# State products of K and V joined to the scores in one TensorE group, with a new order of work, in an mLSTM and hidden-layer kernel

## The chip, the cores and the metric

The kernel runs on one core of one Trainium2 chip. The metric is the device time in microseconds of one execution, taken as the median of several; lower is better. PE is the matrix engine (its weight loads are listed as PEld), DVE, ACT and POOL are the vector, scalar and GpSimd engines, and SP issues the transfers.

## The reference

Two parts follow each other. The first is a gated recurrence (mLSTM) over 768 steps for 4 batches and 8 heads of 40 elements; the second takes its output as 3072 tokens of 320 elements through a hidden layer of 2048.

```python
m_new = np.maximum(f_gate[:, :, t] + m, i_gate[:, :, t])
f_stab = np.exp(f_gate[:, :, t] + m - m_new)
i_stab = np.exp(i_gate[:, :, t] - m_new)
C = f_stab[:, :, None, None] * C + i_stab[:, :, None, None] * np.einsum('bhd,bhe->bhde', vt, kt)
n = f_stab[:, :, None] * n + i_stab[:, :, None] * kt
h_tilde = np.einsum('bhde,bhe->bhd', C, qt)
denom = np.maximum(np.abs(nq), 1.0)          # nq: n times qt
y[:, :, t] = o * h_tilde / denom             # o: sigmoid of o_gate
...
h = x @ w_in
g = h * np.clip(h + 3.0, 0.0, 6.0) / 6.0
return (g @ w_out).astype(np.float32)
```

The weights arrive as 64-bit floats, and the kernel decodes them into 32-bit ones on the chip.

## The kernel before, in words

**Tiling.** The recurrence is computed in chunks of 128 steps: 6 chunks a batch, 24 in all, each in two halves of four heads. Three chunks make a unit (u = 0 to 7), and a unit has two tasks, one for each four heads. For each chunk of a task there are these jobs:

- `state` (L547): the state product of K and the weighted V of the chunk, four pairs of matrix products into a PSUM bank of its own (tile `c`, L559). DVE and POOL then make the new state `C` from the old one: POOL multiplies by the decay (L567), DVE adds (L569).
- `gate` (L574): the decay matrix `gw`. For the first two chunks it is made on PE by products with a selector `sel` (tile `gb`, L589) and a minimum with a mask on DVE (L591); for all others, four rows `gsc` are fetched by a broadcast transfer (L596) and masked on POOL (L598). ACT then takes the exponential, one head at a time (L603).
- `front` (L607): scores of q and k (L624) and q times the old state (L627), both into one bank (tile `s`). DVE multiplies the scores by `gw` (L632) and the state part by `eG` (L638). From task 4 on (PT = 4) the product is split into three bf16 parts (L643 to L650).
- `back` (L657): the product with V into tile `o`, in fp32 before task PT (L669) and as 16 bf16 products from it on (L671 to L674), added into `ht` on DVE.

`fin` (L691) normalises, multiplies by the output gate, transposes on PE (tile `x`, L726) and writes the unit's input of the hidden layer as a high and a low part, `xh` and `xl`.

**Hidden layer.** For every unit there are 16 hidden blocks `h` (`mm1`, L825, eight products of 384 columns each), each followed by the activation on ACT (L839) and DVE (L841), and, for two blocks at a time, the second product into three accumulators `acc` (`mm2`). Unit 0 uses fp32 weights `vr` there (L866), the others high and low parts (L868 to L870). The low part of `g` is made by ACT and DVE (L353, L849).

**Weights.** There are 8 slices of `w_in` (`yi`) and 8 of `w_out` (`yo`); `weight_slice` (L741) decodes one: ACT scales both halves (L752, L754), DVE clamps (L757), shifts (L759) and merges sign and bits (L761), and POOL adds the low half (L766 for `vr`, L768 for `yi`). From `yi` the parts `whi`, `wlo` and `wtl` follow.

**Order.** All engines work through lists that are fixed when the program is built. A planner (class `Plan`) draws them up: every job has a due time (`due`, with the constants from `SPAN` to `FIN0`), asks in turn for an engine with an assumed cost, and the planner gives an engine to the job that is due first of those that can start. In front of the hidden layer it fills PE with dummy products `pw` (`warm`, L373), as a job of lowest rank, or of the highest where the columns of the last 3.4 us fall below `RATE`. The letter at each place of `ENGINES` says which engines an operation may go to. Waits in the lists are on semaphores, so an engine whose next entry isn't ready stands still, with all that follows it.

## Time and profile before

| | |
|---|---|
| median of 3 runs | 510.04 us (509.13 to 510.32) |
| the profiled execution | 509.07 us |
| its span in the profile | 507.3 us |
| PE, DVE, ACT, POOL busy | 499.5, 355.2, 300.4, 159.3 us |
| first hidden product starts | 50.34 us |
| last product starts | 503.62 us |
| dummy products `pw` | 363 |

The span runs from the first to the last instruction of the program; the device time has some 1.8 us around it. A row of the timeline gives start, duration, engine, line, what is written from what is read, shapes and count; matrix products overlap, so the distance between two starts, not the duration, is what one costs PE. An fp32 product has two records.

### The profile page before, as it was taken

The page shows a single profiled execution, that of the slowest core. Times are in us where ns is not written, and L with a number is a line of the kernel's source. Part 1 is how long each engine was busy: PE and PEld are TensorE (multiplying, and loading weights), DVE is VectorE, ACT ScalarE, POOL GpSimd, SP SyncE. Part 2 cuts the span into 40 slices and gives each one's busy share as a digit, 9 for nine tenths or more (in the row PEclk, how much of TensorE's full clock was granted, in tenths as well). Part 3 has the DMA queues.
Part 4 walks back from the last instruction along what each step waited for, and adds up shares of the span by engine and source line. Part 5 has one row for each costly group of instructions (what it writes and reads, how often), then busy time and mean ns, then how long its engine had stood idle before and what let it go on. Part 6 is the DMA issues. An engine that isn't in the chain of part 4 may idle for free.

```text
span 507.3 us, 10993 instructions
## 1 busy us (share of the span) xinstructions
PE 499.5 (98%) x4293; PEld 463.4 (91%) x4293; DVE 355.2 (70%) x754; ACT 300.4 (59%) x649; POOL 159.3 (31%) x195
## 2 busy tenths in 40 slices
PE   8998999999999999999999999999999999999997
PEld 8998877878999999999999999999999999999996
DVE  7879999999856776666767775765866676743332
ACT  4755566767566765657655766647665664443333
POOL 4552454465433333314431333304331331000000
PEclk9998999999999999999999999999999999999999
DMA  8755755624131532215120432215221310001001
GB/s 290 253 219 160 258 196 199 231 81 122 64 103 63 141 109 74 78 44 168 63 97 33 137 111 74 84 42 165 79 82 23 121 61 1 1 0 40 1 1 40
DMA packets 25332, 52.13 MB, mean 103 GB/s; under 512 B 2624, under 2 KB 9088, under 8 KB 25280
## 3 DMA queue, kind: packets, MB, share of 16 engines
q1 hardware_dynamic: 25280, 51.42, 31.5%
q8 instruction: 34, 0.56, 0.4%
q14 instruction: 18, 0.15, 0.1%
HBM read 47.38 MB, written 4.03 MB: 101 GB/s over the span
## 4 chain that ended last, share of the span: by engine, by line
PE 86%; DVE 8%; DMA 2%; issue 2%; ACT 1%; POOL 1%; SPq 0%; DVEq 0%; POOLq 0%
PE h L825 34%; PE acc L868 11%; PE acc L870 10%; PE acc L869 10%; PE s L624 5%; PE pw L373 3%; PE acc L866 3%; PE c L559 2%; PE s L627 2%; PE x L726 1%; PE o L671 1%; PE o L673 1%; DMA gw<-gsc 1%; DVE wlo L784 1%; DVE g L841 1%
## 5 line engine op out<-in xcount | busy, mean ns | idle before, releaser
L839 ACT ACTIVATE g<-h,half 128x384 f32<-128x384 f32 x128 | 74.0, 578 | 86.0 <-PE h L825 84.9
L841 DVE SCALAR_TENSOR_TENSOR g<-g,h 128x384 f32<-128x384 f32 x128 | 70.3, 550 | 63.7 <-ACT g L839 62.9
L868 PE MATMUL acc<-vh,gh 128*128 128x320 f32 x336 | 107.2, 319 | 0.0
L870 PE MATMUL acc<-vh,gl 128*128 128x320 f32 x336 | 104.1, 310 | 0.0
L869 PE MATMUL acc<-vl,gh 128*128 128x320 f32 x336 | 104.0, 310 | 0.0
L849 DVE TENSOR_TENSOR gl<-g,gh 128x384 fp32r<-128x384 f32 x112 | 74.8, 668 | 32.8 <-ACT gh L353 32.2
L825 PE MATMUL h<-xh,whi 128*128 128x384 f32 x256 | 94.5, 369 | 0.1
L825 PE MATMUL h<-xh,wlo 128*128 128x384 f32 x256 | 86.6, 338 | 0.0
L825 PE MATMUL h<-xl,whi 128*128 128x384 f32 x256 | 86.5, 338 | 0.0
L353 ACT CAST gh<-g 128x384 fp32r<-128x384 f32 x112 | 57.2, 511 | 43.2 <-DVE g L841 42.3
L650 POOL TENSOR_TENSOR p<-gw,p 128x512 bf16<-128x512 f32 x36 | 44.4, 1232 | 103.0 <-ACT p L353 96.8
L603 ACT ACTIVATE gw<-gw,cT 128x128 f32<-128x128 f32 x192 | 65.7, 394 | 14.4 <-POOL gw L598 11.9
L598 POOL TENSOR_SCALAR_AFFINE_SELECT gw<-gw 128x512 f32<-128x512 f32 x46 | 33.9, 736 | 110.7 <-DMA gw<-gsc 99.9
L868 PEld LDWEIGHTS acc<-vh,gh 128*128 128x128 f32 x336 | 63.1, 188 | 0.9
L869 PEld LDWEIGHTS acc<-vl,gh 128*128 128x128 f32 x336 | 63.2, 188 | 0.0
L870 PEld LDWEIGHTS acc<-vh,gl 128*128 128x128 f32 x336 | 63.1, 188 | 0.0
L353 ACT CAST p<-gw 128x512 bf16<-128x512 f32 x72 | 44.3, 615 | 19.9 <-DVE gw L632 17.7
L825 PEld LDWEIGHTS h<-xh,whi 128*128 128x128 f32 x256 | 48.0, 188 | 4.4 <-DVE g L841 1.2
L825 PEld LDWEIGHTS h<-xl,whi 128*128 128x128 f32 x256 | 48.3, 189 | 0.2
L825 PEld LDWEIGHTS h<-xh,wlo 128*128 128x128 f32 x256 | 48.1, 188 | 0.0
L825 PE MATMUL h<-xh,wtl 128*128 128x384 f32 x128 | 43.3, 338 | 0.0
L825 PE MATMUL h<-xl,wtl 128*128 128x384 f32 x128 | 43.2, 338 | 0.0
(104 smaller groups left out, 884.1 us busy)
## 6 DMA issues: line engine op xcount, KB each, us to landing
st<-in_qk_dram SPq DMA_DIRECT2D x48, 256.0 KB, 2.7
gw<-gsc SPq DMA_DIRECT2D x46, 256.0 KB, 3.3
nat<-in_nat_dram SPq DMA_DIRECT2D x16, 492.0 KB, 4.4
rawi<-in_w_in_dram SPq DMA_DIRECT2D x8, 640.0 KB, 6.0
rawo<-in_w_out_dram SPq DMA_DIRECT2D x8, 640.0 KB, 4.7
on<-in_on_dram SPq DMA_DIRECT2D x8, 480.0 KB, 3.7
out_dram<-ob SPq DMA_DIRECT2D x24, 160.0 KB, 2.2
f_s<-in_fg_dram SPq DMA_DIRECT2D x1, 96.0 KB, 2.1
```

Of the source, the lines that this page charges most:

```text
L353: nc.scalar.copy(dst, src)
L598: nc.gpsimd.affine_select(gw, gw, pattern=[[0, 4], [1, L]], compare_op=ALU.is_ge, fill=NEG, base=0, channel_multiplier=-1)
L603: nc.scalar.activation(gw[:, h, :], gw[:, h, :], AF.Exp, bias=cT[:, c, r0 + h : r0 + h + 1], scale=1.0)
L624: nc.tensor.matmul(sp[:, z, hs], st[rows, 1, hs], st[rows, 0, hs], start=True, stop=True)
L650: E(e).tensor_sub(p[:, 2], gw, p[:, 1])
L825: nc.tensor.matmul(hp, w, x, start=n == 0, stop=n == len(seq) - 1)
L839: nc.scalar.activation(g, hp, AF.Relu, bias=half, scale=1.0 / 6.0)
L841: nc.vector.scalar_tensor_tensor(g, g, 1.0, hp, ALU.min, ALU.mult)
L849: E(e).tensor_sub(gl, g, gh.bitcast(F32))
L868: nc.tensor.matmul(acc, gh[:, ts_], VH[f // 4][:, f % 4, :], start=f == 0, stop=False)
L869: nc.tensor.matmul(acc, gh[:, ts_], VL[p][:, f % 2, :], start=False, stop=False)
L870: nc.tensor.matmul(acc, gl[:, ts_], VH[f // 4][:, f % 4, :], start=False, stop=f == NF - 1)
```

## The change

The state product moves. From unit 1 on (`MS = 1`), `state` is no longer a job of its own: `front` issues the four state products (`outer`), directly ahead of the scores, into 84 free columns of the scores' bank, and makes the new state from there (`update`) behind its two DVE operations; only then is the bank given back. The update is two DVE operations that multiply and add at once, where POOL multiplied and DVE added.

The gate matrices of the first 7 chunks in order, instead of 2, are made on PE. The mask comes in by one more product there, of 512 bf16 columns, and ACT reads PSUM directly, so that the DVE minimum is gone.

Decoding a weight slice takes no add on POOL any more: the low half is scaled to its place by ACT, and two DVE operations shift and merge bits. Weighting V may go to ACT too. `PT` is 6 instead of 4, so tasks 4 and 5 keep fp32 products with V.

The planner's picture of PE is another: a cost for each change of kind (`CHANGE`), a bonus for staying with attention work (`STICK`), a later due time for `back` (`BKO`), waits by the engine that released, and new values of nearly all constants. The lists are therefore in another order everywhere. The file also allows units of other sizes; the list used is eight times three, as before.

On PE, in unit 2 of the hidden layer, around the state product of task 7, chunk 1 (`c7_1` before; `h2_3` is hidden block 3 of unit 2, `o7_0` a product with V), the list before reads

```order
L825 MATMUL h2_3_2595<-xh2_1927,wtl_77 128x384
L825 MATMUL h2_3_2595<-xl2_1928,wtl_77 128x384
L559 MATMUL c7_1_2635<-vp7_2375,nat7_2372 64x42 x4
L825 MATMUL h2_4_2684<-xh2_1927,whi_75 128x384
L825 MATMUL h2_4_2684<-xl2_1928,whi_75 128x384
```

and now

```order
L894 MATMUL h2_6_2499<-xh2_1679,wtl_77 128x384
L894 MATMUL h2_6_2499<-xl2_1680,wtl_77 128x384
L610 MATMUL s7_1_2533<-vp7_2326,nat7_2315 64x42 x4
L693 MATMUL s7_1_2533<-st7_1_1796 128x128 x4
L696 MATMUL s7_1_2533<-C7_0_2456,st7_1_1796 128x42 x4
L743 LDWEIGHTS p7_0_2463
L743 MATMUL o7_0_2547<-vb7_2327,p7_0_2463 128x84
```

The state product stood alone between two hidden blocks; it now writes into the scores' tile and the scores follow it, and behind them the product with V of the chunk before.

On PE in the start-up, the first gate matrices (`gb`), the list before reads

```order
L589 MATMUL gb0_0_187<-g_s_97,sel_102 128x128 x4
L452 MATMUL pl0_226<-gTs_99,last_98 128x32
L624 MATMUL s0_0_159<-st0_0_108 128x128 x4
L589 MATMUL gb0_1_219<-g_s_97,sel_102 128x128 x4
L430 MATMUL pc1_234<-ident_78,i_s_94 128x32
```

and now

```order
L652 MATMUL gb0_0_220<-mask_102,identb_103 128x512
L654 MATMUL gb0_0_220<-g_s_97,sel_101 128x128 x4
L693 MATMUL s0_0_154<-st0_0_108 128x128 x4
L502 MATMUL pc0_205<-gTs_99,last_98 128x32
L652 LDWEIGHTS identb_103
L652 MATMUL gb1_0_221<-mask_102,identb_103 128x512
L654 MATMUL gb1_0_221<-g_s_97,sel_101 128x128 x4
```

Each gate has a mask product ahead of its four selector products, and the second gate is that of task 1.

On DVE, where the hidden layer of unit 0 begins (`yo` and `yi` are weight slices, `g0_0` the first hidden block's activation, `xl0` the last part of its input), the list before reads

```order
L732 TENSOR_TENSOR xl0_651<-x2_1_2_949,xh0_650 128x128
L638 TENSOR_TENSOR ht2_787<-s2_1_886,eG_82 128x168
L761 SCALAR_TENSOR_TENSOR yi3_522<-rawi3_434,yi3_522 128x640
L757 TENSOR_SCALAR yo0_847<-yo0_847 128x640
L757 TENSOR_SCALAR yi4_934<-yi4_934 128x640
L759 TENSOR_SCALAR yo0_847<-yo0_847 128x640
L759 TENSOR_SCALAR yi4_934<-yi4_934 128x640
L841 SCALAR_TENSOR_TENSOR g0_0_1013<-g0_0_1013,h0_0_998 128x384
```

and now

```order
L804 TENSOR_TENSOR xl0_503<-x2_1_2_911,xh0_502 128x128
L849 TENSOR_TENSOR wtl_77<-yi3_559,wtl_77 64x128
L850 TENSOR_TENSOR wtl_77<-yi3_559,wtl_77 64x128
L829 TENSOR_SCALAR yo1_746<-yo1_746 128x640
L852 TENSOR_TENSOR wlo_76<-yi3_559,whi_75 128x2x256
L831 SCALAR_TENSOR_TENSOR rawo1_640<-yo1_746,rawo1_640 128x640
L829 TENSOR_SCALAR yi4_800<-yi4_800 128x640
L910 SCALAR_TENSOR_TENSOR g0_0_974<-g0_0_974,h0_0_962 128x384
```

At the same point one slice of each kind more is decoded, and the three DVE operations of a slice are a clamp and two merges.

The diff, cut to its core:

```diff
-SWITCH = 0.12
+SWITCH = 0.13
+MS = 1
+BKO = 9.255
+CHANGE = {"moe": 0.085, ("moe", "front"): 0.092, ("moe", "state"): 0.092, ("back", "front"): 0.085, ("fin", "front"): 0.095, ("back", "state"): 0.085, ("fin", "state"): 0.095, ("front", "moe"): 0.105, ("state", "moe"): 0.106}
+STICK = 39.626
-PT = 4
-GB = 2
+PT = 6
+GB = 7
-GP = [1, 1, 4]
+GP = [1, 2, 3]
-RATE = 3500
+RATE = 4500
...
+                if e == "p" and self.last != "moe" and j["gen"].__name__ not in ("mm1", "mm2", "warm"):
+                    due -= STICK
...
-                    if big and self.small:
-                        cost = cost + 0.08
+                    if kind != self.last:
+                        cost = cost.plus(CHANGE.get((self.last, kind), CHANGE.get(kind, 0.0)))
...
+    def outer(task, cp, cps):
+        for h in range(4):
+            z, j = divmod(h, 2)
+            nc.tensor.matmul(cps[z * HR : z * HR + HR, j, :], tasks[task]["kn"](cp, h), tasks[task]["vp"][:, cp, h, :], start=True, stop=True)
+
+    def update(task, cp, cps):
...
+            q0 = (r0 // 4) * 2
+            yield "d", 0.33
+            for k in range(2):
+                nc.vector.scalar_tensor_tensor(Cn[:, k, :], cur[:, k, :], dec[:, c, q0 + k : q0 + k + 1], cps[:, k, :], ALU.mult, ALU.add)
...
-                nc.tensor.matmul(cps[z * HR : z * HR + HR, j, :], T["kn"](cp, h), T["vp"][:, cp, h, :], start=True, stop=True)
...
-                e = yield psub(16, 84)
-                q0 = (r0 // 4) * 2
-                E(e).tensor_tensor(Cn, cur, dec[:, c, q0 : q0 + 2, None].broadcast_to([128, 2, E2]), ALU.mult)
-                yield "d", cd(84)
-                nc.vector.tensor_add(Cn, Cn, cps)
...
+            nc.tensor.matmul(src, GT["identb"], mask[:, None, :].broadcast_to([128, 4, L]), start=True, stop=False)
             for h in range(4):
-                nc.tensor.matmul(pb[:, h, :], sel[:, h, :], g_s[:, c * L : (c + 1) * L], start=True, stop=True)
-            yield "d", cd(512)
-            nc.vector.tensor_tensor(gw, pb, mask[:, None, :].broadcast_to([128, 4, L]), ALU.min)
-            put(*gb)
+                nc.tensor.matmul(src[:, h, :], sel[:, r0 + h, :], g_s[:, c * L : (c + 1) * L], start=False, stop=h == 3)
...
+        both = u >= MS and c < NC - 1
+        cost = pair(4, L).plus(SWITCH) if cur is None else pair(4, L) + pair(4, E2).plus(SWITCH)
+        yield "p", KV + cost if both else cost
+        if both:
+            cps = sp[:, 0, 2 * L + 2 * E2 : 2 * L + 4 * E2].rearrange("p (j e) -> p j e", j=2)
+            outer(task, cp, cps)
...
+        if both:
+            yield from update(task, cp, cps)
         put(*got)
+        if u >= MS:
+            event(f"state{nm}")
...
-        e = yield pick(15, d=lf(WC), g=1.0)
-        E(e).tensor_scalar(y, y, 3, None, ALU.logical_shift_left)
-        yield "d", ld(WC)
-        nc.vector.scalar_tensor_tensor(y, hw, 0x80000000, y, ALU.bitwise_and, ALU.bitwise_or)
-        yield "g", cg(WC)
+        yield "d", Lock(0.765)
+        nc.vector.scalar_tensor_tensor(lw, y, 3, lw, ALU.logical_shift_left, ALU.bitwise_or)
...
-            nc.gpsimd.tensor_tensor(VR[i].rearrange("p a d -> p (a d)"), y, lw, ALU.add)
-        else:
-            nc.gpsimd.tensor_tensor(y, y, lw, ALU.add)
+        yield "d", Lock(0.765)
+        nc.vector.scalar_tensor_tensor(VR[i].rearrange("p a d -> p (a d)") if kind == "o" else y, hw, 0x80000000, lw, ALU.bitwise_and, ALU.bitwise_or)
```

More of the change, by code (lines that the diff above doesn't have):

```diff
@@ L139, in add @@
         self.n += 1
-        self.waiting.append(dict(due=due, n=self.n, gen=gen, t=0.0, eng=None, req=None, after=list(after), att=att, slack=DELTA if slack is None else slack, first=slack is not None, hot=hot))
+        j = dict(due=due, n=self.n, gen=gen, t=At({}), eng=None, req=None, after=list(after), need=set(after), att=att, slack=DELTA if slack is None else slack, first=slack is not None, hot=hot)
+        self.left += 1
+        for a in j["need"]:
+            self.waiting.setdefault(a, []).append(j)
+        if not j["need"]:
+            self.fresh.append(j)
     def put(self, tag, slot):
@@ L212, in ready @@
     def ready(self, j, e, cost):
[L213 removed]
+        start = self.free[e]
+        for o, t in j["t"].by.items():
+            t += (HOPS if e in "dag" else 0.0) if o == e else HOPP if e == "p" and j["att"] and o != "t" else HOP
+            if t > start:
+                start = t
         if e == "g" or isinstance(cost, Lock):
@@ L267, in run @@
             self.settle()
-        assert not self.waiting, [(w["n"], w["due"], w["after"]) for w in self.waiting]
+        assert not self.left, sorted(self.waiting)
 def ca(n):
@@ L375, in mlstm_moe_kernel @@
     GT = {k: early["ea"].tile(sh, F32, name=k) for k, sh in dict(
-        f_s=[BH, S], i_s=[BH, S], m_s=[BH, S], lf=[BH, S], g_s=[128, S], last=[128, 128], gTs=[128, NC, BH], mask=[128, L], one=[BH, L], sel=[128, 4, L]).items()}
+        f_s=[BH, S], i_s=[BH, S], m_s=[BH, S], lf=[BH, S], g_s=[128, S], last=[128, 128], gTs=[128, NC, BH], one=[BH, L], sel=[128, 8, L]).items()}
+    GT.update({k: early["ea"].tile([128, L], BF16, name=k) for k in ("mask", "identb")})
     def load_ident():
@@ L855, in mm2 @@
         native = u < NV
-        for t in range(U):
+        for t in range(UNITS[u]):
             if p == 0:
@@ L975, in _layout @@
     vp[..., D] = 1.0
+    kc, vc = chunks(k), chunks(vp)
+    both = np.concatenate([kc, vc], 3)
+    nat = units(both, lambda a: np.stack([np.concatenate([a[:, q, :, : 4 * D].transpose(1, 0, 2).reshape(L, -1), a[:, q, :, 4 * D :].transpose(1, 0, 2).reshape(L, -1)], 1) for q in range(2)]))
     w1, w2 = moe_w_in.view(np.int64), moe_w_out.view(np.int64)
```

402 lines of the change are left out of this document (227 added, 175 removed).

## The prediction

> **What bounds the kernel now.** I read the page's shares first, then the stretches of the span, then the chain that ended last.
>
> ```profile
> PE 499.5 (98%) x4293; PEld 463.4 (91%) x4293; DVE 355.2 (70%) x754; ACT 300.4 (59%) x649; POOL 159.3 (31%) x195
> ...
> PE 86%; DVE 8%; DMA 2%; issue 2%; ACT 1%; POOL 1%; SPq 0%; DVEq 0%; POOLq 0%
> ```
> ```profile
> 0.00:49.50 49.50, 46.59 (x627) 43.60 (x628) 40.22 (x114) 27.60 (x73) 22.95 (x38) 0.97 0.70 235
> 49.50:110.00 60.50, 58.94 (x387) 48.99 (x385) 57.99 (x114) 41.16 (x79) 30.50 (x28) 1.00 0.59 199
> 110.00:507.30 397.30, 393.93 (x3284) 370.80 (x3282) 256.95 (x529) 231.65 (x498) 105.84 (x131) 1.00 0.23 72
> ```
>
> The columns of the second fence are PE, PEld, DVE, ACT, POOL, clock, DMA share and GB/s. There are three stages. Up to 50 us the attention of unit 0 is prepared and PE is filled up with dummy products; DVE is busy 40 of 49.5 us. From 50 to 110 us the hidden layer of unit 0 runs while the weights are still being decoded; PE (58.9 of 60.5) and DVE (58.0) are both full. After 110 us only PE counts: it loses nothing until the final copy and store. So the time is (start of the first hidden product) + (PE work behind it) + (waits of PE) + (the tail behind the last product). The start is at 50.34 us:
>
> ```profile
> 48.74 1.53 PE L373 MATMUL pw<-ones 128*128 128x128 bf16 x19
> 50.34 0.44 PE L825 MATMUL h<-xh,whi 128*128 128x384 f32 x1
> ```
>
> **The joined state products.** Busy rows overlap on PE, so I price by distances between starts. A state product that stands alone between hidden products reads:
>
> ```profile
> 186.63 0.34 PE L825 MATMUL h<-xh,wtl 128*128 128x384 f32 x1
> 186.81 0.34 PE L825 MATMUL h<-xl,wtl 128*128 128x384 f32 x1
> 187.08 0.44 PE L559 MATMUL c<-vp,nat 128*64 128x42 f32 x8
> 187.45 0.44 PE L825 MATMUL h<-xh,whi 128*128 128x384 f32 x1
> 187.73 0.34 PE L825 MATMUL h<-xl,whi 128*128 128x384 f32 x1
> ```
>
> Hidden products follow each other at 0.175 us (186.63 to 186.81 is one such step). Going into the state product takes 0.27, so 0.095 more; the state product itself 0.37; the first hidden product behind it takes 0.28, so 0.105 more. Standing alone costs 0.20 us. Where before happens to have state and scores next to each other:
>
> ```profile
> 107.83 0.44 PE L559 MATMUL c<-vp,nat 128*64 128x42 f32 x8
> 108.20 0.72 PE L624 MATMUL s<-st 64*128 64x128 f32 x8
> 108.75 0.54 PE L627 MATMUL s<-C,st 64*128 64x42 f32 x8
> 109.22 0.44 PE L825 MATMUL h<-xh,whi 128*128 128x384 f32 x1
> 109.50 0.34 PE L825 MATMUL h<-xl,whi 128*128 128x384 f32 x1
> ```
>
> the state product is again 0.37 and the scores' 0.55 is not lengthened, so the join is free. Behind the first hidden product the old order has 32 state products, 29 of them with dense work next; the new one has 32, all with scores next: 29 x 0.20 = -5.8 us. The other kinds are regrouped too: attention pieces between dense work fall from 107 to 70, so 8 more go than the 29. They are mostly P x V products, which now stand behind the scores. One of them saves about its exit and that of the scores in front, 0.1 each, and some of this is given back where scores used to follow P x V: -1.0 us for these, an estimate between 0 and -1.6 (8 x 0.20). Together -6.8.
>
> The Trainium skill, TensorEngine Tiling (Array Packing), Tiling Modes, says that a change of tiling mode drains TensorE, and state product (128x64) and scores (64x128) are different modes; by that rule 32 joins would each pay a change again, about 3.2 us at the 0.10 of the rows. The trace does not agree: 107.83 to 108.75 shows no such time.
>
> **P x V of two more tasks in fp32.** Tasks 4 and 5 leave the bf16 split.
>
> ```profile
> 51.85 0.98 PE L669 MATMUL o<-nat,gw 128*128 128x42 f32 x8
> 52.66 0.42 PE L825 MATMUL h<-xh,whi 128*128 128x384 f32 x1
> ...
> 181.21 0.21 PE L671 MATMUL o<-vb,p 128*128 128x84 bf16 x1
> ...
> 181.81 0.71 PE L624 MATMUL s<-st 64*128 64x128 f32 x8
> ```
>
> 0.81 us against 0.60, of which 0.08 is the change to scores: +0.29 x 6 = +1.7 on PE. The casts and subtractions that go leave ACT, DVE and POOL, which have room there. One chunk's scores (0.55 and 0.47 by 108.20 to 109.22) and one P x V (0.81) move ahead of the first hidden product: -1.8 behind it. These two cancel: -0.1.
>
> **The start.** Seven gate matrices are now made on PE instead of two.
>
> ```profile
> 6.59 1.11 PE L589 MATMUL gb<-g_s,sel 128*128 128x128 f32 x8
> 7.61 0.38 PE L452 MATMUL pl<-gTs,last 128*128 128x32 f32 x2
> ...
> 17.93 6.03 PE L373 MATMUL pw<-ones 128*128 128x128 bf16 x105
> 23.89 0.44 PE L559 MATMUL c<-vp,nat 128*64 128x42 f32 x8
> ...
> 42.17 0.72 PE L373 MATMUL pw<-ones 128*128 128x128 bf16 x10
> 44.03 1.09 PE L669 MATMUL o<-nat,gw 128*128 128x42 f32 x8 [1.14 <-DVE C L569]
> ...
> 46.83 1.91 PE L373 MATMUL pw<-ones 128*128 128x128 bf16 x16
> 48.53 0.42 PE L726 MATMUL x<-ident,on 128*128 128x128 f32 x1
> ```
>
> Five more gates at 1.02 are +5.1. Seven mask products of 512 bf16 columns have no row; 128 columns cost 0.057 (5.96 / 105), so four times that, 0.22, is the lower end and twice that (half clock) the upper; at 0.22 they are +1.6. The chunk moved forward is +1.8. Dummy products fall from 363 to 270: -93 x 0.057 = -5.3. With the waits of before, PE would start at 50.3 + 3.2 = 53.5. Those waits are some 4 us: about 3 us in all stood idle (1.14 here, 0.31 for the first scores, the rest in pieces), and the 16 dummy products from 46.83 run at 0.106, half clock, which over 46 to 49.3 us lost 1.5. With none of it the start is 49.2. The gate path is what I expect to shorten them: the chain of waits holds a gate's DMA that starts at 30.41 and lasts 5.33 us, and then POOL and ACT.
>
> ```profile
> 30.41 5.33 DMA gw<-gsc
> ```
>
> The gates of unit 0 no longer go that way. DVE decides against it: in the part before the start it has five weight slices begun or done (three operations each) instead of four, and the add that POOL did is now a DVE operation.
>
> ```profile
> 50.46 0.49 DVE L757 TENSOR_SCALAR yo<-yo 128x640 f32<-128x640 f32 x1
> 50.86 1.88 DVE L757 TENSOR_SCALAR yi<-yi 128x640 f32<-128x640 f32 x1
> 52.66 0.48 DVE L759 TENSOR_SCALAR yo<-yo 128x640 uint32<-128x640 uint32 x1
> ...
> 54.17 0.81 DVE L761 SCALAR_TENSOR_TENSOR yo<-rawo,yo 128x640 uint32<-128x640 uint32 x1
> 54.96 0.55 DVE L841 SCALAR_TENSOR_TENSOR g<-g,h 128x384 f32<-128x384 f32 x1
> ```
>
> By 0.40 and 0.8 per operation that is +4.4, and the rest of DVE's list before the start is about even. DVE's idle time there, 49.5 - 40.2 = 9.3 us, must take this; 3.6 of it lies before the first gate data. So DVE gives 49 to 54.7, the same bracket as PE. I take 51.5, the middle: +1.2.
>
> **Waits behind the start.** Per slice DVE now does 0.40 + 0.8 + 0.8 instead of 0.40 + 0.40 + 0.8: +0.4 for 11 or 12 slices. But POOL loses its adds:
>
> ```profile
> L766 POOL TENSOR_TENSOR vr<-yo,rawo 128x640 uint32<-128x640 uint32 x8 | 13.5, 1685 | 15.2 <-issue 5.3 <-ACT whi L353 3.1 <-ACT rawo L754 2.9
> L768 POOL TENSOR_TENSOR yi<-yi,rawi 128x640 uint32<-128x640 uint32 x8 | 13.3, 1667 | 9.1 <-DVE yi L761 8.2 <-ACT gw L603 0.8
> ```
>
> 26.8 us of POOL go, and with them the hold-ups of DVE such as the 1.88 at 50.86 (its twin at 50.46 took 0.40), which ran beside a POOL add. The chain no longer passes POOL between decode and second product either. PE's row for 49.5 to 110 leaves 1.6 us idle, and with what its overlapping ends hide I put the waits of this stage at 1.9; I take 1.0 now, bounds 0 and 4 (0.4 x 11 not hidden at all). Elsewhere, three hidden blocks in a row occur four times more, and the third waits:
>
> ```profile
> 474.55 0.34 PE L825 MATMUL h<-xl,wtl 128*128 128x384 f32 x1
> 474.80 0.45 PE L825 MATMUL h<-xh,whi 128*128 128x384 f32 x1
> 475.08 0.34 PE L825 MATMUL h<-xl,whi 128*128 128x384 f32 x1
> ```
>
> 0.25 + 0.28 against 2 x 0.175 is +0.18, four times +0.7. Sum of waits -0.2. The state update is now two DVE operations behind the gate product and holds the only score bank longer, by about 0.3 (nearest row: the C add, 0.24 busy); scores are some 8 us apart in the last stage, so this is hidden there. End of the program: the same order of the last products and stores, nothing.
>
> **Sum.** 507.3 - 6.8 - 0.1 + 1.2 - 0.2 = 501.4 us of span. The profiled execution took 509.07, 1.8 more than its span: 503.2. The median of the runs is 510.04, about 1 above the profiled one: 504.
>
> **Rivals.** *The start is late.* The waits stay and PE falls to half clock once more: start at 53.5 + 1.7, time 504 + 3.7 = 507.7. For it: fewer dummy products, DVE with more work. Against: the gate DMAs go. The 1.7 is the loss of one such piece like 46 to 49.3 us. The Trainium skill, TensorE: Matmul & The Clock Gate, Part 1, gives a window of about 3.4 us after which an idle PE is put to half rate; the rows at 46.83 agree with such a length.
>
> *The join is not free.* Entry or exit is paid again inside the group, 32 x 0.1: 504 + 3.2 = 507.2, the change doing half of what it says. For it: only three joins stand behind the start in the trace. Against: they, and four ahead of the start, are all at 0.37.
>
> *Slower: the shared bank.* State product and scores wait together for the weighted V and for the one score bank, which DVE frees only after the update. Between 50 and 110 us DVE is full; if each of the nine groups there makes PE wait 1.1 us (as the P x V at 44.03 waited 1.14 for a state update), that is +10: 514. It turns the sign above 0.6 us per group. For it: DVE 58.0 of 60.5. Against: POOL's load goes, and DVE's list from the start to the last slice is no longer than before: it has fewer weight slices left and 14 of the hidden layer's `g` operations in it instead of 17.
>
> *Better.* Start at 49.2 and no waits to 110 us: 500.7.
>
> **Chances.** Forecast 0.60 (its own range 501.5 to 506.5), late start 0.12, join not free 0.07, these two together (504 + 3.7 + 3.2 = 510.9) 0.07, shared bank 0.07, better 0.07. The predicted time is 504; the range, 500.5 to 508.5, leaves out the two together and the shared bank. A measurement can tell 0.2%, so no change is 509.0 to 511.1: faster 0.60 + 0.12 + 0.07 + 0.07 = 0.86, same 0.07, slower 0.07.
>
> **What would show it.** Right: the first hidden product at 50 to 53; state product to scores 0.37 and scores unchanged; no idle PE behind 110 us; POOL nearly empty in 50 to 110. Wrong: a start above 54 (the start step), more than 0.4 us from state product to scores (the join), PE waits at scores for DVE's state update (the bank).

## The result, and the profile after

The changed kernel takes 505.82 us (median; 505.24 to 506.39), the kernel before, run beside it, 509.64 us (509.13 to 510.32): ratio 0.9924, 95% interval 0.9904 to 0.9944. A second series gave 505.72 us and 0.9932 (0.9911 to 0.9952). It is faster by 3.8 us. The forecast was 504.0 from 510.04, so 6 us. The profiled execution took 505.40 us, its span is 503.7 us. The page of the changed kernel (busy time, then the shares of the chain that ended last, by engine and by line), the chain of the kernel before by line, and the three stretches of the changed kernel (PE, PEld, DVE, ACT, POOL, granted clock, DMA share, GB/s):

```profile
PE 494.5 (98%) x4199; PEld 465.3 (92%) x4199; DVE 356.1 (71%) x839; ACT 262.3 (52%) x606; POOL 95.2 (19%) x117
...
PE 82%; DVE 5%; DMA 5%; ACT 3%; POOL 2%; issue 1%; POOLq 0%; SPq 0%; ACTq 0%; DVEq 0%
PE h L894 31%; PE acc L937 9%; PE acc L939 9%; PE acc L938 9%; PE s L693 5%; DMA gw<-gsc 5%; PE acc L935 4%; PE o L741 3%; PE s L696 3%; PE s L610 2%; PE x L798 2%; PE pw L424 1%; ACT gw L666 1%; PE o L743 1%; PE gb L654 1%
```
```profile
PE h L825 34%; PE acc L868 11%; PE acc L870 10%; PE acc L869 10%; PE s L624 5%; PE pw L373 3%; PE acc L866 3%; PE c L559 2%; PE s L627 2%; PE x L726 1%; PE o L671 1%; PE o L673 1%; DMA gw<-gsc 1%; DVE wlo L784 1%; DVE g L841 1%
```
```profile
0.00:50.50 50.50, 47.46 (x616) 44.38 (x616) 42.86 (x128) 32.13 (x92) 12.88 (x23) 1.00 0.71 228
50.50:110.00 59.50, 58.01 (x365) 49.36 (x366) 54.01 (x113) 39.12 (x81) 4.74 (x7) 1.00 0.58 186
110.00:503.70 393.70, 389.04 (x3220) 371.57 (x3218) 259.20 (x599) 191.07 (x435) 77.62 (x87) 1.00 0.24 72
```

PE's work has gone down, and GpSimd is nearly empty from 50 to 110 us (4.7 us busy, 30.5 before). But in the chain PE's share fell from 86 to 82%, and `DMA gw<-gsc`, the fetch of a gate matrix from DRAM, rose from 1% to 5%. Behind 110 us PE now leaves 4.7 us idle (393.70 - 389.04); before, 3.4, which was the tail. The overlapping ends of PE's rows hide most of its waits.

The join itself reads as forecast. One group of the changed kernel, on PE:

```profile
136.32 0.34 PE L894 MATMUL h<-xl,wtl 128*128 128x384 f32 x1
136.59 0.44 PE L610 MATMUL s<-vp,nat 128*64 128x42 f32 x8
136.96 0.71 PE L693 MATMUL s<-st 64*128 64x128 f32 x8
137.50 0.54 PE L696 MATMUL s<-C,st 64*128 64x42 f32 x8
137.98 0.30 PE L741 MATMUL o<-nat,gw 128*128 128x42 f32 x1
```

State product to scores 0.37 us, scores 0.54, as in the old trace where the two happened to be neighbours.

To part work from waiting I took, for every block of PE (products of one kind in a row), the distance from its start to the next block's start, less the usual distance for that block between those neighbours in the kernel before. What is left over counts as waiting; the rest of the time between the first hidden product and the last product is PE work. Kernels with the same products in the same order come out at the same PE work within 0.1 us, which is how far this can be trusted. All kernels of this study, each from its one profile, the time and ratio from all its runs:

| kernel | time, us | ratio to before (95%) | first hidden product | PE work behind it | waits to 110 us | waits 110 to 440 us |
|---|---|---|---|---|---|---|
| before | 509.64 | 1 | 50.3 | 450.5 | 1.9 | -0.1 |
| changed | 505.82 | 0.9924 (0.9904-0.9944) | 50.5 | 443.7 | 1.2 | 3.9 |
| changed_again | 505.72 | 0.9932 (0.9911-0.9952) | 50.4 | 443.7 | 1.5 | 6.8 |
| apart20 | 509.41 | 0.998 (0.9962-0.9998) | 51.8 | 447.6 | 1.6 | 3.0 |
| states_apart_replanned | 510.44 | 1.0003 (0.9981-1.0024) | 52.9 | 442.5 | 4.0 | 7.8 |
| states_apart_gate4 | 505.73 | 0.9923 (0.9908-0.9938) | 51.4 | 442.5 | 4.5 | 2.5 |
| reorder4 | 506.63 | 0.9927 (0.9906-0.9948) | 50.6 | 443.7 | 3.6 | 3.4 |
| gate4 | 501.81 | 0.983 (0.9805-0.9855) | 49.3 | 443.7 | 1.2 | 1.3 |
| gate5 | 501.41 | 0.9842 (0.9829-0.9855) | 49.4 | 443.7 | 1.1 | 1.8 |
| gate4_moves | 500.5 | 0.9816 (0.9789-0.9843) | 49.4 | 443.7 | 0.6 | 0.9 |
| before_gate4 | 509.19 | 0.999 (0.9981-0.9998) | 49.2 | 450.5 | 3.1 | 0.0 |
| planner_fetch | 502.46 | 0.9854 (0.9829-0.9879) | 49.9 | 445.6 | -0.1 | 0.7 |
| planner_fetch_32 | 506.63 | 0.9945 (0.9923-0.9967) | 53.7 | 443.2 | 2.5 | 0.7 |
| planner_gate4 | 511.5 | 1.0021 (1.0001-1.0041) | 57.1 | 442.8 | 3.5 | 2.4 |

A profile caught one execution, not the median one: 508.48 us for changed_again, 507.41 for reorder4, 513.17 for states_apart_replanned. In these three, PE ran at half clock for 3.4 us behind the first hidden product, up to 1.7 us (half of it) that the table counts as waiting (up to 110 us in reorder4, later in the other two).

The last stretch, 440 us to the end, waits 0.9 us in all of them. So the changed kernel has 6.8 us less PE work, a start 0.2 later, 0.7 us less of waiting up to 110 us, and 3.9 us of waiting between 110 and 440 us, where PE had not waited at all.

### The profile page after: what moved, and what is told of

It reads as the page before. It is cut to its first block, busy times and chain, and to the rows that moved or that the text cites. A ratio compares the mean times of both kernels' runs of the same rounds, so it can differ in the third digit from the quotient of the medians.

```text
span 503.7 us, 10688 instructions
## 1 busy us (share of the span) xinstructions
PE 494.5 (98%) x4199; PEld 465.3 (92%) x4199; DVE 356.1 (71%) x839; ACT 262.3 (52%) x606; POOL 95.2 (19%) x117
## 4 chain that ended last, share of the span: by engine, by line
PE 82%; DVE 5%; DMA 5%; ACT 3%; POOL 2%; issue 1%; POOLq 0%; SPq 0%; ACTq 0%; DVEq 0%
PE h L894 31%; PE acc L937 9%; PE acc L939 9%; PE acc L938 9%; PE s L693 5%; DMA gw<-gsc 5%; PE acc L935 4%; PE o L741 3%; PE s L696 3%; PE s L610 2%; PE x L798 2%; PE pw L424 1%; ACT gw L666 1%; PE o L743 1%; PE gb L654 1%
## 5 line engine op out<-in xcount | busy, mean ns | idle before, releaser
L908 ACT ACTIVATE g<-h,half 128x384 f32<-128x384 f32 x128 | 73.7, 576 | 109.3 <-PE h L894 101.9
L894 PE MATMUL h<-xh,whi 128*128 128x384 f32 x256 | 92.3, 361 | 0.6 <-DVE g L910 0.5
L918 DVE TENSOR_TENSOR gl<-g,gh 128x384 fp32r<-128x384 f32 x112 | 66.1, 593 | 20.9 <-ACT gh L403 19.6
L403 ACT CAST gh<-g 128x384 fp32r<-128x384 f32 x112 | 57.1, 510 | 44.0 <-DVE g L910 43.7
L666 ACT ACTIVATE gw<-gw,cT 128x128 f32<-128x128 f32 x164 | 54.2, 392 | 43.2 <-POOL gw L660 43.1
L660 POOL TENSOR_SCALAR_AFFINE_SELECT gw<-gw 128x512 f32<-128x512 f32 x41 | 29.4, 716 | 209.1 <-DMA gw<-gsc 140.9
L719 POOL TENSOR_TENSOR gw<-gw,p 128x512 f32<-128x512 f32 x30 | 35.0, 1166 | 85.7 <-DVE p L405 80.0
L701 DVE TENSOR_TENSOR gw<-s,gw 128x512 f32<-128x512 f32 x48 | 32.9, 687 | 7.2 <-PE s L696 6.4
```

The lines of the kernel that those rows point to most:

```text
L403: nc.scalar.copy(dst, src)
L660: nc.gpsimd.affine_select(gw, gw, pattern=[[0, 4], [1, L]], compare_op=ALU.is_ge, fill=NEG, base=0, channel_multiplier=-1)
L666: nc.scalar.activation(gw[:, h, :], src[:, h, :], AF.Exp, bias=cT[:, c, r0 + h : r0 + h + 1], scale=1.0)
L701: nc.vector.tensor_tensor(gw.rearrange("p (z j) l -> p z (j l)", z=2), sp[:, :, : 2 * L], gw.rearrange("p (z j) l -> p z (j l)", z=2), ALU ...
L719: E(e).tensor_sub(gw, gw, p[:, 0])
L894: nc.tensor.matmul(hp, w, x, start=n == 0, stop=n == len(seq) - 1)
```

## Where the new waits hang

The chain of waits of the changed kernel, before the transposes `x` at 358 us (start, duration, what):

```profile
350.47 0.70 DVE p L723
351.17 0.02 SPq L658
351.19 0.03 issue
351.22 3.94 DMA gw<-gsc
...
355.32 0.09 POOL gw L660
...
355.91 1.46 POOL nat L596
...
357.40 0.62 ACT vb L403
...
358.04 0.68 DVE vb L600
358.73 0.08 DVE rd L779
358.81 0.59 DVE gw L701
```

Read from the top: VectorE's last remainder of P (L723) frees one of three gate buffers; only then does SyncE issue the next fetch; 3.94 us later GpSimd masks the gate matrix (L660), and the remainder of V (L596), which needs no gate, stands behind that mask in GpSimd's queue. ScalarE's and VectorE's steps on V follow, and the outputs that PE is to transpose stand behind those on VectorE. This gate matrix is ready 15.8 us before its scores use it: nothing waits for the gate, everything waits behind it. The same shape on ScalarE, at the second place:

```profile
139.14 3.89 DMA gw<-gsc
...
143.19 0.63 POOL gw L660
...
144.15 0.68 ACT gw L666 x2
144.83 0.47 ACT g L908
...
145.33 0.56 DVE g L910
...
145.94 1.16 PE h L894 x5
```

Here the buffers are freed by the P x V products of task 5, which in fp32 read the gate buffer itself; a hidden block's first step on ScalarE (L908) stood behind the exponentials. SyncE's waits for a gate buffer from 128 to 150 us (us in total, times, longest):

```profile
SPq L658 <- PE o L741: 7.1, 3, 5.9
```

Two of the three, 0.6 us each, stand ahead of fetches of this chain, issued at 133.79 and 139.14 us. The longest belongs to the next fetch, issued at 145.49.

And the largest of its waits over the whole span, the changed kernel's first and then the kernel before's:

```profile
SPq L658 <- DVE p L723: 135.4, 26, 11.9
```
```profile
SPq L596 <- POOL p L650: 107.7, 25, 12.7
```

Both kernels hold the fetch back for more than half of the gate matrices that come this way (26 of 41 and 25 of 46 by these rows alone). So the hold alone does not cost time: PE waits -0.1 us between 110 and 440 us in the kernel before. What differs is what stands behind it.

## The experiments

In the kernels that keep an order, the planner's decisions are replaced by the recorded list of the decisions of the changed kernel (or of the one named), so that no instruction moves except those that the edit names.

**apart20: twenty joins undone, order held.**

```diff
-        yield "p", KV + cost if both else cost
+        apart = both and (task, cp) in APART
+        yield "p", KV if apart else KV + cost if both else cost
         if both:
...
             outer(task, cp, cps)
+        if apart:
+            yield "p", cost
```

> The changed kernel with its order of work held as it is, but for 20 of the 32 joined groups: there the state products are taken out of the group and put one hidden block (or one set of six output products) ahead of it, where a full-array product stands on both sides. Theory 'the join pays by itself': a state product that stands alone costs 0.20 us more than one that runs into the scores (entry 0.095 + exit 0.105), so 20 x 0.20 = 4.0 us more PE work: about 509.8 us against the 505.8 of the changed kernel, and the state product to next product 0.57 us at these 20 places against 0.37 in the group. Rival 'the gain came from the new order of work, the join is incidental': less than 1 us more, below 506.8.

509.41 us, +3.6. The PE work is 447.6 against 443.7: 3.8 us before rounding, for 20, 0.19 each. (Two of the 20 come to stand behind a P x V product and not between dense work; over the other 18 it is 0.21.) One of the twenty:

```profile
136.91 0.34 PE L898 MATMUL h<-xl,wtl 128*128 128x384 f32 x1
137.18 0.44 PE L611 MATMUL s<-vp,nat 128*64 128x42 f32 x8
137.55 0.44 PE L898 MATMUL h<-xh,whi 128*128 128x384 f32 x1
137.83 0.34 PE L898 MATMUL h<-xl,whi 128*128 128x384 f32 x1
```

0.27 into it, 0.37, and 0.28 for the first hidden product behind it: the price of the prediction. The rival falls.

**states_apart_replanned: the joined form off, planned anew.**

```diff
-MS = 1
+MS = 8
```

> The changed kernel with all state products as steps of their own in banks of their own again (the joined form off), planned anew by the changed planner with its rule that groups pieces of other kinds. In the order that comes out 21 of 32 state products still stand beside scores or transposes, 11 alone, and PE goes over 76 times from the hidden and output products to another kind (70 with the join, 107 in the kernel before). Theory 'what pays is that a state product stands beside other small products, by whatever means': 11 x 0.20 = 2.2 us at most of the join's 5.8 are lost, and by the spacings of the kernel before the PE work comes out within 1 us of the changed kernel: 505.5 to 508 us. Rival 'the joined form in one bank is what pays': all of it is lost, 511 us or more.

510.44 us, nearly the rival's number, but not for its reason. The PE work is 442.5 us, as the first theory had it. One chunk more lies ahead of the first hidden product, 1.8 us by the prediction's rows; with it, PE work is 0.6 us above the joined kernel's, not 5.8. State products set beside other small products are nearly as good as joined. The time went into waits, 12.6 us in all, and a start 2.3 us later. Neither theory had that. The profile is of the longest of twelve executions (513.17), and these waits contain a piece at half clock from 128.7 us:

```profile
128.00:134.00 6.00, 6.00 (x37) 5.76 (x35) 3.31 (x7) 4.07 (x11) 0.64 (x1) 0.72 0.13 34
```

**gate4: a fourth gate buffer, order held.** (rank counts the gate matrices; GB is 7.)

```diff
-                     egw=EGW, y=NY, ...
+                     egw=EGW, gx=1, y=NY, ...
...
-        got = yield ("get", "gw", "egw") if u == 0 else ("get", "gw")
+        got = yield ("get", "gw", "egw") if u == 0 else ("get", "gw", "gx") if rank[task, cp] > GB else ("get", "gw")
```

> The changed kernel in its own order on every engine, with a fourth buffer for the gate matrices from the ninth of them on, so that a gate matrix can be fetched before a product has freed one of three. Theory 'late gate matrices': most of the PE waits that are new behind the first hidden product (1.26 us before the transposes at 61.4, 0.66 before the hidden block at 146, 0.36 and 0.68 before the transposes at 244 and 358) end a chain that starts with the fetch of a gate matrix held back for a buffer; with the buffer they go, 1.7 to 2.9 us: 503 to 504 us. Rival 'VectorE and ScalarE are simply too busy now that PE has less to do': the waits stay, less than 0.5 us gained, 505.3 us or more.

501.81 us: 4 us less than the changed kernel with not one instruction moved, and more than either theory gave. The waits between 110 and 440 us fall from 3.9 to 1.3; those before the transposes at 244 and 358 us and in the P x V products at 236 and 351 us are gone, that at 61 us falls from 1.26 to 0.70, that at 144 from 0.66 to 0.37; one at 81 us grows from 0.36 to 1.15. The rest came from the start, which I had not counted: 49.3 us against 50.5 (49.4 in both other kernels with the added buffer and this order). SyncE's waits for L723, 135.4 us in 26 times in the changed kernel, are now:

```profile
SPq L658 <- DVE p L723: 3.5, 1, 3.5
```

**gate5: five buffers** (gx=2).

> The changed kernel in its own order with five buffers for the gate matrices. Theory 'in-order queues behind a gate matrix held back for a buffer': the fourth buffer took the waits at 146, 236, 244, 351 and 358 us; what was left with it (0.7 before the transposes at 61, 1.1 at 81, 0.4 at 144 us) falls again by 0.5 to 1.5 us: 500.5 to 501.5 us. Rival 'with four buffers the fetch is bound by the order of SyncE's queue or by VectorE': no further gain, 501.5 to 502.2 us.

501.41 us, as with four. The median lies 0.1 us inside the first theory's range and decides nothing, but the trace agrees with the rival: SyncE's rows name no wait for L723 any more, and PE's waits behind the start are 3.8 us in all, where they were 3.4 with four buffers. What is left does not come from buffers.

**before_gate4: the same buffer in the kernel before, its own order held.**

> The kernel before, in its own order on every engine, with the fourth buffer for the gate matrices from the ninth of them on. Theory 'the changed order made the wait for a gate buffer': in the kernel before, PE waits 2.8 us behind the first hidden product, none of it between 110 and 440 us, so a buffer more can take little: 509 to 510 us, less than 1 us gained (1.9 of the 2.8 us lie between 60 and 110 us, where gate matrices are fetched too, so up to 1.5 us if these hang on the same chain). Rival 'three buffers were always too few': about the 4 us that the changed kernel gained, 506 us.

509.19 us, 0.3 less. The start came 1.1 us earlier and was given back: waits up to 110 us went from 1.9 to 3.1, where VectorE decodes weights. The old order has nothing to gain from the buffer behind the start, so the waits between 110 and 440 us belong to the new order.

**states_apart_gate4: the same buffer in the replanned kernel with separate state products, its order held.**

> The replanned kernel with the state products as steps of their own, in the order that it had at 510.4 us, with the fourth buffer for the gate matrices. Its PE waits behind the first hidden product were 12.6 us by the spacings of the kernel before, its PE work without them 442.5 us (443.7 in the changed kernel). Theory 'the waits of that order come from held-back gate matrices too': 4 us or more go, 506.5 us or less, and the joined form has no part in what is left. Rival 'they come from the state products' own banks and buffers' (the rows name a state product's load as the waiting one): less than 2 us, 508.5 us or more.

505.73 us, 4.7 less (4.1 by the ratios to the kernel before), by the first theory. Waits between 110 and 440 us fall from 7.8 to 2.5; up to 1.7 us of that fall is the half-clock piece, which this profile does not have. But about 4.5 us of waits stay between the start and 110 us, and one row names the state product itself:

```profile
PE acc L935 <- DVE g L910: 1.9, 2, 1.4
PE h L894 <- DVE g L910: 1.1, 2, 0.8
PE c L610 <- DVE ht L757: 1.0, 1, 1.0
```

It is 3.9 us slower than gate4, with 1.2 us less PE work behind the start and one chunk, 1.8 us, more ahead of it. What saves PE time is that small products stand together, by joining or by the order; whether the joined form helps the waits, or only this order has more of them, stays open.

**reorder4: three buffers, instructions moved ahead of work that waits for a gate matrix.** As the order of the engines shows it (GpSimd; one of the two places), then VectorE at 61 us:

```
+L596 TENSOR_TENSOR nat_3095<-nat_3095,vb_3107 128x504
 L660 AFFINE_SELECT gw_2_3140<-gw_2_3140 128x512
-L596 TENSOR_TENSOR nat_3095<-nat_3095,vb_3107 128x504
...
+L787 TENSOR_TENSOR on_926<-on_926,rd_0_1025 128x3x160
 L864 TENSOR_TENSOR vl_1060<-vr_660,vh_1059 128x640
-L787 TENSOR_TENSOR on_926<-on_926,rd_0_1025 128x3x160
```

> The changed kernel with the same buffers and the same order on PE, and five instructions moved up past work that waits for a late gate matrix: GpSimd's remainder of V ahead of the masking of a gate matrix (tasks 9 and 13), ScalarE's first step of a hidden block ahead of the gate exponentials at 144 us, VectorE's two gating products of the outputs ahead of a split of the output weights at 61 and at 82 us. Theory 'work queued in order behind a late gate matrix': the transposes' waits at 61, 82, 244 and 358 us and the hidden block's at 146 go, 1.2 + 0.3 + 0.36 + 0.68 + 0.5 = 3.0 us: about 502.8 us. Rival 'the engines are too busy': the waits move on to the next piece, less than 0.8 us gained, 505 us or more.

506.63 us: a miss. The order shows six moved instructions, not five: at 82 us both gating products moved, the second ahead of a hidden block's `g`. The waits at 61 us (1.26 to 0.10) and 146 us went, those at 244 and 358 us fell only from 0.36 to 0.16 and from 0.68 to 0.53, and others came: 0.49 and 0.48 at 64 and 65 us, 0.71 at 353, and 1.69 at 68 us, where the granted clock (eighth column) fell:

```profile
66.00:68.00 2.00, 1.69 (x28) 1.55 (x28) 2.00 (x6) 0.33 (x1) 0.00 (x0) 1.00 0.03 8
68.00:70.00 2.00, 2.00 (x10) 1.36 (x9) 2.00 (x5) 0.00 (x0) 0.00 (x0) 0.62 0.70 169
70.00:72.00 2.00, 2.00 (x6) 1.22 (x5) 2.00 (x5) 0.98 (x2) 0.00 (x0) 0.53 0.97 281
```

At 356 us the remainder of V, first in GpSimd's queue now, waited for ScalarE's rounding of V instead:

```profile
POOL nat L596 <- ACT vb L403: 4.1, 1, 4.1
```

Two of the six executions have a mean granted clock of 0.996 or 0.997; the other four took 505.83 to 506.9, so the clock is not what kept the gain away. I read this as: while the fetch is held back, several queues have work behind it, and a step moved up in one meets the next. The rival's number fits, its reason does not: gate4 shows that the engines are not too busy.

**gate4_moves: with the fourth buffer, two steps of ScalarE moved up.**

```
+L403 CAST vh_1060<-vr_661 128x640
 L666 ACTIVATE gw_2_851<-gw_2_851,cT 128x128 x2
-L403 CAST vh_1060<-vr_661 128x640
```

> The changed kernel in its own order with the fourth buffer, and two steps of ScalarE moved up: the rounding of the first output weights ahead of the last two gate exponentials in front of it (about 58 us), and the first step of hidden block 7 of unit 1 ahead of four gate exponentials (about 143 us). With the buffer alone PE still waits 0.70 us before the transposes at 61 us and 0.4 to 0.8 us at 144 us. Theory 'what is left are places in the in-order queues': both waits go, about 1.0 us: 500.8 us. Rival 'moved work only moves the wait', as the five moves without the buffer did: 501.4 to 502 us as with the buffer alone.

500.5 us (499.18 to 502.36). In the trace three gate exponentials, not four, stood ahead of the second step. In its profile both waits are gone (0.70 and 0.37 us), the waits of all stages are 2.4 us, 1.0 less than gate4's. The times of gate4, gate5 and gate4_moves overlap, so by time it is not shown to be faster than these, though its median is the lowest here; that the two waits went rests on one profile.

**changed_again: the changed kernel once more.**

> The changed kernel once more, beside the others on the same chip. Theory and rival alike: 505.8 us as before (ratio 0.992); it shows how far the first hidden product's start (50.54 us in its first profile, 51.8 and 50.6 in two kernels with the same order up to there, 49.3 with the fourth buffer) moves from run to run with nothing changed: by less than 0.5 us if the fourth buffer's 1.2 us at the start are its own, by 1 us or more if they are chance.

505.72 us, and the start at 50.4. Four starts in this order with three buffers are 50.4, 50.5, 50.6 and 51.8 (apart20), three with an added buffer 49.3, 49.4 and 49.4. They do not overlap, and the kernel before went from 50.3 to 49.2 with the buffer; but the spread of the four is as large as the difference, so its size is not fixed by these. Its profile caught the longest of six executions (508.48; the others 504.86 to 506.63), and shows what that one lost:

```profile
349.00:351.00 2.00, 1.49 (x9) 1.16 (x7) 1.34 (x5) 1.75 (x5) 0.00 (x0) 1.00 0.08 29
351.00:353.00 2.00, 0.44 (x3) 0.21 (x3) 1.27 (x4) 0.00 (x0) 1.15 (x1) 1.00 0.87 200
353.00:355.00 2.00, 1.57 (x18) 1.57 (x19) 1.65 (x5) 1.13 (x4) 0.00 (x0) 0.86 0.79 299
355.00:357.00 2.00, 2.00 (x9) 2.00 (x8) 1.27 (x4) 2.00 (x7) 0.00 (x0) 0.50 0.31 104
357.00:360.00 3.00, 3.00 (x24) 2.80 (x23) 2.74 (x5) 2.25 (x7) 2.06 (x2) 0.86 0.00 0
```

PE was busy 1.9 of 4 us from 349 to 353, at a place where the chain again starts with a gate's fetch, and then ran at half clock for 3.4 us in all: by the rows' mean clocks (0.86, 0.50, 0.86) for 0.28 of the first 2 us, for all of the next 2 and for 0.28 of the last 3. By the spacings the waits cost 3.0 us and the clock 1.6 more. The mean granted clock of this execution is 0.997, of the other five 0.999 to 1.0. The Trainium skill, TensorE: Matmul & The Clock Gate, Part 1, says that the gate has two states, half and full rate, decided by a free-running window of about 3.4 us; the 0.50 and the 3.4 us agree. That the window runs free would let the same shortage cost a half-clock piece in one execution and none in another; no run here shows it.

**planner_fetch: the planner books more time for every load, near the true one for a gate's fetch,** three buffers, planned anew.

```diff
-DMA0 = 0.65
+DMA0 = 2.0
```

> The changed kernel planned anew with one number changed: the planner books 1.35 us more for every load, so 3.4 us for a gate matrix from issue to landing where it had 2.0; the trace of the changed kernel shows 3.3 (median of 41, 3.0 to 5.6). Three buffers as before. The order that comes out has 74 pieces between hidden and output products, one chunk less ahead of the first hidden product, and PE work behind that product of 445.8 us by the spacings of the kernel before (443.9 in the changed kernel). Theory 'the planner sets urgent work behind a fetch that it takes for too short': told the truth it avoids this, PE waits behind the first hidden product fall from 6.0 to 3.5 us or less, and the time is 445.8 + 3.5 + 49.5 (start) + 5.3 (tail and what lies around the span) = 504 us. Rival 'the hold-up is the buffer, which the planner already counts; a new order comes out with waits of its own': 6 us of waits or more, 506.5 us or more.

502.46 us, the first theory, and better than its number: 1.5 us of waits in all, 0.9 of them in the last stretch, where three hidden blocks stand in a row. No wait of PE is left in the rows of waits, and from 50 to 110 us it is full:

```profile
49.80:110.00 60.20, 60.14 (x390) 50.73 (x390) 54.98 (x119) 42.37 (x91) 8.79 (x10) 1.00 0.61 206
```

SyncE holds the fetches back nearly as long as in the changed kernel, so here too it is what stands behind them that changed:

```profile
SPq L658 <- DVE p L723: 115.4, 26, 7.7
```

It is ahead of the changed kernel by more than 3 us although PE has 1.9 us more work behind the start.

**planner_fetch_32: nearly the same booked time** (DMA0 = 1.8).

> The changed kernel planned anew with 1.15 us more booked for every load, 3.2 us for a gate matrix instead of 3.4: near the same truth, and another order: 72 pieces, the same chunks ahead of the first hidden product as in the changed kernel, 443.4 us of PE work behind it by the spacings of the kernel before, 344 dummy products. Theory 'a booked fetch near the real one keeps urgent work from behind a fetch': PE waits of 3 us or less, 443.4 + 2.5 + 50 + 5.3 = 501 us. Rival 'the low waits at 3.4 us were the luck of one order': 6 us or more of waits, 504.7 us or more.

506.63 us: a miss in time. The mechanism held where it was found (0.7 us of waits between 110 and 440 us, as with 3.4 us booked), but this order starts its first hidden product at 53.7 us and waits 2.5 us up to 110. Its waits, 4.1 us in all, lie between the two theories' numbers. Both plans with the longer booked time wait little in the long stage; the start and the decode stage come out of each new plan differently.

**planner_gate4: four buffers that the planner knows of, planned anew, fetch booked short as in the changed kernel.**

```diff
-NGW = 3
+NGW = 4
```

> The changed kernel planned anew with four buffers for the gate matrices from the start, known to the planner. Its order has 69 pieces and 442.9 us of PE work behind the first hidden product by the spacings of the kernel before. Theory 'with the buffer there the waits stay low in any order of this planner': 4 us of waits or less, 442.9 + 4 + 50 + 5.3 = 502 us. Rival 'the order that comes out decides, the buffer helps only the order that happened to be held up': 6 us of waits or more, 504.5 us or more.

511.5 us, the worst miss: 0.2% slower than the kernel before, barely clear of the noise, with less PE work behind the start than the changed one. The start came at 57.1 us. The chain ahead of it:

```profile
29.25 0.33 SPq L658
...
30.15 6.96 DMA nat<-in_nat_dram
...
37.13 0.34 ACT vp L575
...
37.51 0.97 PE s L610 x8
```
```profile
SPq L658 <- DVE gw L701: 4.2, 1, 4.2
SPq L658 <- PE o L741: 4.2, 1, 4.2
```

The load of K and V for a whole task stood behind a gate's fetch on SyncE, and that fetch stood 8.4 us (the second fence, SyncE's waits from 24 to 31 us, one after the other at the same fetch); in the changed kernel a load of this kind left at 26.74 us. The weighted V (L575) and the state product (L610) waited for it, and the chain to the first hidden product runs on from there. A buffer more does not help a plan that has filled it in advance and put a more urgent load behind the next fetch. The Trainium skill, DMA: Bandwidth & Descriptors, Anatomy of one DMA, says, in a section on the GpSimd path, that a transfer's wait is served by the issuing engine and not by the DMA; these rows on SPq agree.

## Why the prediction was right or wrong

The direction and the range held; the time came 1.8 us above the forecast. That it came so near is in part luck: PE work was right within 0.1 us, the waits behind the start were 3.4 us worse than forecast, and the start (1.0), the tail (0.2) and the step from span to median (0.5) came out better. By the terms of the sum:

- **Joined state products and regrouping, -6.8; fp32 and moved chunk, -0.1.** Measured together -6.8 (450.5 to 443.7). Each join is worth 0.19 (apart20), 0.20 by the prediction, so 29 of them make 5.5, an estimate; the runs do not part the remaining 1.3. The joined form is not needed for most of it: with separate state products, 21 of 32 set beside scores or transposes by the planner, PE's work is 0.6 us more in all.
- **A price for the change from state product to scores** (3.2 us for 32 joins) did not show: 0.37 in 31 of the 32 groups behind the start; the other one, at 127.73 us, took 0.76.
- **The start, +1.2.** Measured +0.2, and the bracket of 49.2 to 53.5 held, but not by the reason given. By the distances between starts gates and masks cost 5.9 us more and not 6.7 (five more gates 0.87 each, a mask 0.22), and the small transposes and products around them 1.7 us instead of 2.5, which the sum left out. The idle time that the prediction saw shrink with "the gate DMAs go" did not: PE stood 2.9 us idle before its start in the kernel before (the row below) and 3.0 in the changed one (50.50 - 47.46). What went is the piece at half clock at 46 us, with a mean clock of 0.97 before and 1.00 now:

```profile
0.00:50.30 50.30, 47.37 (x638) 44.21 (x638) 41.02 (x115) 28.40 (x75) 23.07 (x38) 0.97 0.69 231
```

This is not one profile's chance: 44 of the 69 executions of the kernel before that ran beside the experiments have a mean clock of 0.997 or less over the whole kernel, and one of ten of the changed kernel. VectorE's +4.4 is 3.6 by the prediction's own prices (five slices at 2.0 us less four at 1.6), which leaves the middle of its bracket near 51.5. With the fourth buffer the start came at 49.3, so a part of the start's waits probably hung on a gate buffer too.
- **Waits behind the start, -0.2.** This is the step that failed: measured +3.2. Its two parts were right: the decode stage went from 1.9 to 1.2 (forecast 1.0), and four more third hidden blocks in a row wait 0.19 each, 0.76 (forecast 0.7). What it lacked is 3.1 us between 110 and 440 us. I took from the old profile that PE waits for nothing there, and carried that over to an order in which every engine's queue had been dealt anew. The old profile shows no slack of a queue, only that its order happened to have nothing urgent behind a held-back fetch. One of the prediction's signs of being right, no idle PE behind 110 us, is what failed to come.
- **Rivals.** The late start and the join that is not free did not come. The shared bank did not either: the two groups of task 5 that follow each other at 128 and 131 us wait 0.39 and 0.28 us, no others do, and the rows of waits there name no state update. The case that did come, work queued behind a gate matrix, was not among them, though the prediction quoted the gate's fetch as a piece of the chain in the start (30.41, 5.33 us).
- **From span to median** I added 1.8 and 0.8; it was 1.7 and 0.4.

What the runs settle: 2.6 of the lost 3.1 us come from fetches of gate matrices that are held for a buffer, with work queued behind them in order. One buffer more took them with no instruction moved (gate4), a further one took no more (gate5), and the kernel before, which holds its fetches back as well, gained nothing between 110 and 440 us (before_gate4). That the planner sets urgent work there because it books such a fetch at 2.0 us, where the median is 3.3, is not shown: both plans that booked more wait 0.7 us in the long stage, but each is another order altogether, and the kernel before, whose planner books the same 2.0 us (`DMA0 = 0.65` in both), does not wait there at all. What stays open, then, is which edit made the order prone to it. The chains name two, P x V in fp32 that keeps the gate buffer in tasks 4 and 5, and the last remainder of P, which moved from GpSimd to VectorE and so frees the buffer on another engine than the one that masks the next gate matrix; neither was tried alone, nor were the planner's new constants.

## What to carry to other kernels

The cheapest thing to seek in an order made by a planner is work that needs nothing from a transfer but stands behind it in an in-order queue. The chain of waits names it, and one buffer more, with the order held, was worth about as much here as the whole change (4.0 and 3.8 us). Planned anew, the same buffer lost 5.7 us, and a truer booked time gained 3.4 us in one plan and nothing in another. When a change deals the order anew, price the new waits from the new order; that the old profile has none is no evidence. To measure what one edit is worth, hold the order: new plans of nearly the same kernel came out between 502 and 511 us.

## What was not expected of the hardware

A short shortage of work for PE can cost more than itself. Five of the fourteen traces show such a piece at half clock before the end of the program, each 3.4 us long. In the 3.4 us just ahead of it PE was busy for 1.46 us (changed_again, at 354.5), 2.12 (planner_gate4, at 39.2, and states_apart_replanned, at 128.7), 2.27 (before, at 46.0) and even 2.76 (reorder4, at 68.5, with small products). It does not always follow: in states_apart_gate4 PE was busy for 2.56 of the 4 us from 76 to 80 and kept its full clock.

A gate matrix of 256 KB takes 3.0 to 5.6 us from issue to landing (median 3.3 of 41). And a VectorE operation on 12 columns, in the changed kernel beside GpSimd's remainder of V and without it:

```profile
241.61 1.12 DVE L777 SCALAR_TENSOR_TENSOR rd<-ht 128x12 f32<-128x12 f32 x1
```
```profile
57.03 0.17 DVE L777 SCALAR_TENSOR_TENSOR rd<-ht 128x12 f32<-128x12 f32 x1
```

GpSimd ran its remainder of V from 241.25 us for 1.45 us, so the operation ended 0.03 us behind it; at 57 us GpSimd was idle. Of the 18 such operations of the changed kernel the three that met one of GpSimd's took 0.60, 1.12 and 1.12 us and all ended 0.03 to 0.04 us behind it; the fifteen others took 0.15 to 0.18 us.
